# First feed-forward tile prepared inside the last mixing batch, and the last Fourier parts dealt one tile later

## The chip, the cores and the metric

The kernel runs on one core of one Trainium2 chip. The metric is device time in microseconds of one launch, as the median of three runs. A profile of one execution gives the busy time of each engine: TensorE (PE, with its weight loads as PEld), VectorE (DVE), ScalarE (ACT), GpSimd (POOL), and the DMA queues that SyncE (SP), ACT and POOL issue to.

## The reference, cut to what matters

```python
# q, k, v: (8, 12, 448, 64) float32; w_pre, w_post: (12, 12)
scores = q @ k^T / 8
scores = einsum('bhij,hg->bgij', scores, w_pre)      # mix heads
attn   = softmax(scores, axis=-1)
attn   = einsum('bhij,hg->bgij', attn, w_post)       # mix heads again
x      = (attn @ v) as (8, 448, 768)
u      = x + real(fft(fft(x, axis=1), axis=2))
un     = (u - mean(u)) / sqrt(var(u) + 1e-6)         # per row of 768
out    = u + relu(un @ w_ch1) @ w_ch2                # 768 -> 3072 -> 768
```

The feed-forward weights arrive as 64-bit floats and are turned to 32-bit ones in the kernel. The 8 x 448 = 3584 rows of `u` are 7 feed-forward tiles of 512 rows.

## The kernel before, in words

**Mixing.** `mix_phase` runs over 8 batches of 23 steps, 184 in all. A step takes rows of scores (`Kr`, gathered from `Sb` by SP, L496), mixes heads on PE (premix, L507, into `mx`), takes the maximum (DVE, L514), the exponential (ACT, L521), scales (POOL, L531, two steps ahead of its use), mixes heads again on PE (postmix, L541, into `po`) and transposes on DVE (L554). Products QK (L479) and AV (L571) are interleaved. The attention output of a batch is transposed to rows `X` (L615, PE), folded on POOL (`fold`, L636 to L657: sums and differences of `X` into `xf`), transformed in two products (`emit_z`, L680; `emit_s2`, L696), added to `X` on DVE (L707, L709) and stored as `u` in two scratch tensors, `u_scr` in order and `u_rev` reversed (SP L728, POOL L719, L725). A tile's rows thus come from up to four stretches of a batch.

**What orders the mixing.** `due(kind, step, fn)` puts a piece of work on one of four lists; the main loop takes from them at fixed places of each step (`ORDERS`). Kind "none" is taken at the head of a step, "full" late in it. PE, DVE, ACT and POOL keep this order (`manual_schedule`). A function of kind "none" that returns a true value, as the loads of q and k do, lowers the number of folds in that step from two to one. The last batch begins at step `f = 161`. The loop ends at step 190, and eight Fourier pieces of the last batch (four `z`, four `s2`) with a last flush are left over: they are handed to the next phase as nine `parts`. Raw q and k lie in the pool `praw` (4 buffers), their transposes in `pqt` (4 of `qT`, 4 of `kT`), and PSUM tiles `ms` come from four banks.

**Feed-forward.** `ffn_phase` runs over six chunks `c` of the hidden width and over the seven tiles `t` in each (n = 7c + t); a chunk is computed by a seven-product scheme. `first(n)` has seven steps of 12 products (L1062) into `psP`, `psQ`, `psR`; `second(n)` has seven of 8 products (L1135) for the first two chunks. A tile is loaded (`load_u`, L946), its statistics are taken on DVE (`stats`, L971), the power -0.5 on POOL (`power`, L976 to L979), it is normalised on ACT (`norm`, L987), turned by 24 PE transposes (`turn`, L996, evacuated in L1003) into four half tiles `ub`, and three more `ub` are differences of those (`total`, L1008). Seven `ub` of each tile are stored for later chunks (L1012). For tile 0 all of this stands ahead of `first(0)`; for tile t + 1 it is spread over `first(t)` and `second(t)`. Between tile 0's power and its `norm`, `fold_rest` issues on POOL what folding the last batch has left. `next_part` runs one of the nine parts: before, after five of the seven steps of `first(0)` and after steps of `second(0)`.

**Weights.** `_Weights` converts pieces of the weights: a raw load on POOL (L225), seven DVE operations (L247 to L273), stores (L233). Loads run `ahead` pieces ahead: 4 in the feed-forward phase, with 5 buffers.

**Memory.** Pools of the mixing end with it, and those of the feed-forward phase lie over them: `pub` (11 buffers for `ub`), `pw1`, `pw2`, `ph`, the weight pools, `pun`, and `pu` (3 buffers of 512 rows). PSUM: two banks each for Q, P and R, and two for the leftover parts (`ppx`), which become a third pair (`ppy`) when the parts are done.

Of the kernel before, what the change touches and what calls it, by code (L numbers as in the profile page):

```python
# [16 lines left out]
P = 128  # L17
# [47 lines left out]
C7 = 7  # L65
# [234 lines left out]


@with_exitstack
def mix_phase(ctx, tc, rest, ident, q, k, v, w_pre, w_post, u_scr, u_rev, wts):

# [7 lines left out]
    def pool(name, bufs=1, **kw):  # L312
        return ctx.enter_context(tc.tile_pool(name=name, bufs=bufs, **kw))
# [3 lines left out]

    praw = pool("praw", 4)
    pqt = pool("pqt", 4)
    psb = pool("psb", 2)  # L320
# [415 lines left out]
    def due(kind, at, fn):  # L736
        fill[kind].append((at, len(fill[kind]), fn))
# [4 lines left out]
    for b in range(B):  # L742
# [38 lines left out]
        for pair in range(2):  # L781
            for par in range(2):
                due("full", f + AT_S[pair][par],
                    lambda b=b, pair=pair, par=par: emit_s2(b, pair, par))
    due("none", 0, lambda: wts.deal(0))
    due("none", -39, emit_load_mix)
# [87 lines left out]
OPENS = (0, 1, 4)  # L874
ORDER2 = (0, 3, 5, 6, 4, 1, 2)
DEEP = 2
DEALS = ((0, 2, 2, 2, 2, 0, 0), (2, 3, 3, 3, 3, 0, 0))
# [5 lines left out]
def ffn_phase(ctx, tc, rest, ident, u_scr, u_rev, wts, ub_scr, out, fold_rest,  # L883
              parts):

# [7 lines left out]

    pub = pool("pub", 11)
    pw1 = pool("pw1", 7)
    pw2 = pool("pw2")
    ph = pool("ph")
    wts.open(ctx, tc, 4)
    once = ExitStack()
# [5 lines left out]
    pun = early("pun", 2)  # L905
    pu = early("pu", 3)
    pps = [pool("pps" + k, space=bass.MemoryType.PSUM) for k in "QPR"]
# [16 lines left out]
    def next_part():  # L924
        if parts:
# [6 lines left out]
           for t in range(NTB) for r in range(2) for d in range(2)}  # L932
    mhalf = pst.tile([P, NT2], F32, name="mhalf", bufs=1)
    nc.gpsimd.memset(mhalf[:, :], -0.5)

    def load_u(t):
        us[t] = pu.tile([P, NT2, DM], F32, name="u", tag="u")
        for x in range(NT2):
            p = 0
            while p < P:  # L940
                b, r = divmod(t * TB + x * P + p, S)
                k = sum(r >= e for e in ENDS)
                n = min(P - p, ENDS[k] - r)
                src = (u_rev if k % 2 else u_scr)[b]
                for p0, m in _split(p, n):
                    nc.sync.dma_start(out=us[t][p0:p0 + m, x, :],  # L946
                                      in_=src[r + p0 - p:r + p0 - p + m, :])
                p += n

# [8 lines left out]
    def new_ub(n, i):  # L958
        ubs[n, i] = pub.tile([P, NK, HT], F32, name="ub", tag="ub")


    UB = {(0, 0): 0, (0, 1): 6, (1, 0): 1, (1, 1): 2}

    mvs, uns = {}, {}

    def stats(t, x):
        if x == 0:
            mvs[t] = pst.tile([P, NT2, 3], F32, name="mv", tag="mv", bufs=2)
        st = pst.tile([P, 2, 6], F32, name="st", tag="st")
        for y in range(2):  # L970
            nc.vector.bn_stats(st[:, y, :], us[t][:, x, y * DH:(y + 1) * DH])  # L971
        nc.vector.bn_aggr(mvs[t][:, x, 0:2], st[:, :, :])

    def power(t):
        var = mvs[t][:, :, 1]
        nc.gpsimd.tensor_scalar(var, var, 1e-6, None, op0=ALU.add)  # L976
        nc.gpsimd.tensor_tensor(var, var, mhalf[:, :], op=ALU.pow)
        nc.gpsimd.tensor_tensor(mvs[t][:, :, 2], mvs[t][:, :, 0], var, op=ALU.mult)
        nc.gpsimd.tensor_scalar(mvs[t][:, :, 2], mvs[t][:, :, 2], -1.0, None,  # L979
                                op0=ALU.mult)  # L980

    def norm(t, x):
        if x == 0:
            for i in (0, 6, 1, 2, 4, 5, 3):
                new_ub(t, i)
        uns[x] = pun.tile([P, DM], F32, name="un", tag="un")
        nc.scalar.activation(uns[x][:, :], us[t][:, x, :], ACTF.Identity,  # L987
                             bias=mvs[t][:, x, 2:3], scale=mvs[t][:, x, 1:2])

    def turn(t, x):  # L990
        un = uns.pop(x)
        for y in range(2):
            ps = ps_tile("Q")
            for c in range(NK):
                cc = NK * y + c
                tr = nc.tensor.transpose(ps[:, c * P:(c + 1) * P],  # L996
                                         un[:, cc * P:(cc + 1) * P], ident[:, :])
                if t == x == y == c == 0:

                    tc.keep_in_program_order(tr)  # L1000

            copy = nc.vector.tensor_copy if t == 0 and y else nc.scalar.copy
            copy(out=ubs[t, UB[y, x // 2]][:, :, (x % 2) * P:(x % 2 + 1) * P],  # L1003
                 in_=ps[:, :NK * P].rearrange("p (c n) -> p c n", n=P))

    def total(t, n):
        o, a, b = ((4, 6, 0), (5, 2, 4), (6, 2, 6), (3, 1, 5))[n]
        nc.vector.tensor_tensor(ubs[t, o][:, :, :], ubs[t, a][:, :, :],  # L1008
                                ubs[t, b][:, :, :], op=ALU.subtract)
        if n == 3:  # L1010
            for i in ORDER:
                nc.sync.dma_start(out=ub_scr[t][i], in_=ubs[t, i][:, :, :])  # L1012

# [23 lines left out]
    def first(n, st, beside):  # L1037
# [12 lines left out]
        for k, i in enumerate(ORDER):  # L1050
# [6 lines left out]
            for m in range(FM):  # L1057
                for kc in range(NK):
                    for fn in beside.pop(done, ()):
                        fn()  # L1060
                    done += 1
                    nc.tensor.matmul(p[:, m, :], w1[i][:, kc, m * P:(m + 1) * P],  # L1062
                                     ub[:, kc, :],
                                     start=i in (0, 4, 1)[:3 - seed] and m == kc == 0,
                                     stop=kc == NK - 1, skip_group_check=True)
            if i == 0 and seed:
# [21 lines left out]
            else:  # L1088
                nc.scalar.activation(h12, p, ACTF.Relu)
            if norms and k < NT2:  # L1090
                stats(t + 1, k)
                if k == NT2 - 1:
                    power(t + 1)
            if n == 0 and k not in (1, 2):
                next_part()
# [23 lines left out]
    def second(n, st):  # L1119
# [9 lines left out]
        for k, i in enumerate(ORDER):  # L1129
            for x in range(NT2 // 2):  # L1130
# [9 lines left out]
                if c == 0:  # L1140
                    us_ = u[:, 2 * r + x, d * DH:(d + 1) * DH]
                    nc.vector.tensor_tensor(us_, us_, p, op=ALU.add)
                    if last:
                        nc.sync.dma_start(out=acc[t, r, d][:, x, :], in_=us_)
                    continue
# [17 lines left out]
            if norms and k >= NT2 - 1:  # L1163
                total(t + 1, k - NT2 + 1)
            if n == 0:
                next_part()
# [109 lines left out]

    for t in range(2):
        load_u(t)
    for i in ORDER:
        load_w1(0, i)  # L1280
    ET = mybir.EngineType
    with tc.manual_schedule(engines={ET.PE, ET.DVE, ET.Pool}):
        for x in range(NT2):
            stats(0, x)
        power(0)
        fold_rest()
    with tc.manual_schedule(engines={ET.PE, ET.DVE}):
        for x in range(NT2):
            norm(0, x)
            turn(0, x)  # L1290
        for i in ORDER:
            load_w2(0, i)
        for n in range(4):
            total(0, n)
        parts_ = [(c, k) for c in range(1, NC) for k in range(NK + FM)]
        for n in range(DEEP * NTB):
            c, t = divmod(n, NTB)
            if c == 0 and 0 < t < NK + FM + 1:
                wts.add(*parts_.pop(0))
            while c and sum(o[1] for o in wts.ops) < 52:  # L1300
                wts.add(*parts_.pop(0))
            wts.deal(0)
            if n + 2 < NTB:
                load_u(n + 2)
            st = {}
            first(n, st, {})
            second(n, st)
            if c == 0:
                wts.deal(1000)
            if n == 0:  # L1310
                assert not parts
                rest.close()
                beside.close()
                pps.append(pool("ppy", space=bass.MemoryType.PSUM))
            if n == NTB - 1:
                once.close()
                for name, bufs in (("wt", 1), ("hq", 1), ("od", 9)):
                    right[name] = pool("p" + name, bufs, side="right")
# [29 lines left out]
def kernel(  # L1348
# [19 lines left out]
    ub_scr = [scr.tile([7, P, NK, TB // 2], F32, name=f"ub_{t}") for t in range(NTB)]  # L1368
    wts = _Weights(nc, moe_w_ch1, moe_w_ch2, scr)
    rest = ExitStack()  # L1370
    fold_rest, parts = mix_phase(tc, rest, ident, q, k, v, w_pre, w_post, u_scr, u_rev,
                                 wts)
    ffn_phase(tc, rest, ident, u_scr, u_rev, wts, ub_scr,
              out.rearrange("b s d -> (b s) d"), fold_rest, parts)

# [30 lines left out]
```

## Time and profile before

| what | us |
|---|---|
| median of 3 runs (lowest to highest) | 2374.74 (2374.28 to 2377.43) |
| the profiled execution, whole | 2376.62 |
| its span, first to last instruction | 2374.9 |
| mixing: last matmul ends | 820.7 |
| first product of the feed-forward phase (L1062) starts | 845.6 |
| `second(0)` starts (L1135 in the chain) | 883.4 |
| `first(1)` starts | 908.6 |
| `second(1)` starts | 926.7 |

How to read it: the page gives busy time by engine over the span and in 40 slices of 59.4 us. The first feed-forward tile falls into slices 14 to 16. A group's row gives a line, its engine, what it writes and reads, and the mean time of one instruction; a wait is put down to what came last before the waiting instruction.

### The profile page before, as it was taken

The numbers are of one execution on the slowest core, as the hardware profiler recorded it, in microseconds if no ns is written. First come the engines' busy times: TensorE is split into PE (matmuls) and PEld (weight loads), VectorE is DVE, ScalarE is ACT, GpSimd is POOL, SyncE is SP. The second block draws the span as 40 slices with busy tenths as digits, with TensorE's granted clock in tenths as the row PEclk, the third lists the DMA queues.
The fourth block names the chain that finished last, engine by engine and source line by source line (L and its number), as shares of the span: only waits on it lengthen the run. The fifth ranks groups of instructions, "written<-read, shape, count | busy, mean of one in ns | idle before, by whom it ended". The sixth has DMA issues, their size and how long they took to land.

```text
span 2374.9 us, 59455 instructions
## 1 busy us (share of the span) xinstructions
PE 2282.5 (96%) x22600; PEld 1716.0 (72%) x22600; DVE 1677.3 (71%) x3596; ACT 1102.4 (46%) x3085; POOL 1130.8 (48%) x1680
## 2 busy tenths in 40 slices
PE   6999999999999769999999999999999999999998
PEld 2455555555555457767777779999899999999997
DVE  3768877787877547786676766778767777776556
ACT  4766766666676422222122224443444444344444
POOL 3587867878777341121234443335333433443333
PEclk9999999999999979999999999999999999999999
DMA  7565555656645636666888895569456846674553
GB/s 160 156 181 175 174 178 154 202 160 181 189 148 171 216 106 205 193 217 239 229 238 231 206 299 140 147 168 272 128 140 180 238 129 178 167 221 113 147 128 66
DMA packets 213625, 425.60 MB, mean 179 GB/s; under 512 B 39014, under 2 KB 135678, under 8 KB 213342
## 3 DMA queue, kind: packets, MB, share of 16 engines
q1 hardware_dynamic: 142430, 280.35, 34.4%
q0 software_dynamic: 64912, 139.48, 27.0%
q8 instruction: 181, 2.97, 0.5%
q10 hardware_dynamic: 6000, 1.97, 0.5%
q14 instruction: 102, 0.84, 0.1%
HBM read 213.16 MB, written 129.39 MB: 144 GB/s over the span
## 4 chain that ended last, share of the span: by engine, by line
PE 76%; issue 7%; DMA 5%; POOL 4%; DVE 4%; ACT 3%; SPq 1%; ACTq 0%; POOLq 0%; DVEq 0%
PE psP L1062 15%; PE psP L1192 10%; PE psR L1062 8%; PE mx L507 6%; PE psR L1192 5%; PE ms L571 5%; PE ms L479 5%; PE psQ L1062 4%; PE po L541 4%; PE psP L1135 4%; DMA Kr<-Sb 3%; PE psQ L1192 2%; PE psR L1135 2%; PE ms L696 2%; ACT PP L521 1%
## 5 line engine op out<-in xcount | busy, mean ns | idle before, releaser
L1062 PE MATMUL psP<-ub,w1t 128*128 128x256 f32 x2016 | 480.5, 379 | 1.3 <-DVE h L1081 1.3
L1062 PEld LDWEIGHTS psP<-ub,w1t 128*128 128x128 f32 x2016 | 379.0, 190 | 49.5 <-DVE h L1081 1.7
L531 POOL TENSOR_SCALAR PP<-PP,rcp 128x448 f32<-128x448 f32 x368 | 234.5, 647 | 214.7 <-DVE rcp L529 172.7
L521 ACT ACTIVATE PP<-mx,nmx 128x448 f32<-128x448 f32 x368 | 230.3, 631 | 189.6 <-DVE nmx L514 177.4
L514 DVE TENSOR_REDUCE nmx<-mx 128x1 f32<-128x448 f32 x368 | 214.1, 619 | 134.8 <-PE mx L507 132.1
L1226 POOL DMA_DIRECT2D out_dram<-od x109 | 133.1, 1427 | 281.9 <-DVE od L1223 159.5
L1026 POOL TENSOR_TENSOR hq<-h 128x256 f32<-128x256 f32 (+1 forms) x168 | 104.6, 622 | 291.0 <-ACT h L1082 171.6
L1062 PE MATMUL psR<-ub,w1t 128*128 128x256 f32 x1008 | 232.9, 381 | 0.0
L507 PE MATMUL mx<-Kr,kw 60*32 60x448 f32 x2944 | 213.4, 550 | 14.1 <-DMA Kr<-Sb 12.3
L1223 DVE TENSOR_TENSOR od<-od 128x768 f32<-128x768 f32 x196 | 188.9, 975 | 52.5 <-ACT od L1220 50.7
L1062 PEld LDWEIGHTS psR<-ub,w1t 128*128 128x128 f32 x1008 | 192.6, 191 | 26.4
L479 PE MATMUL ms<-kT,qT 64*32 64x448 f32 (+1 forms) x3072 | 202.4, 547 | 9.3 <-ACT qT L342 6.6
L554 DVE STREAM_TRANSPOSE Pv<-po 128x896 f32<-128x896 f32 x184 | 203.7, 1107 | 7.5 <-PE po L541 3.7
L342 ACT COPY Sb<-ms 124x448 f32<-124x448 f32 (+1 forms) x384 | 184.4, 540 | 39.5 <-PE ms L479 24.5
L541 PE MATMUL po<-PP,kw 60*32 60x448 f32 x2944 | 197.1, 541 | 0.3 <-DVE rcp L528 0.2
L1220 ACT COPY od<-psP 128x192 f32<-128x192 f32 x390 | 124.7, 320 | 145.5 <-PE psP L1192 141.1
L571 PEld LDWEIGHTS ms<-Pv,vv 64*64 64x64 f32 x5376 | 137.4, 132 | 69.0 <-issue 48.9
L225 POOL DMA_DIRECT2D raw<-in_moe_w_ch_dram x88 | 53.2, 605 | 262.9 <-DVE tmp L269 256.8
L571 PE MATMUL ms<-Pv,vv 64*64 64x120 f32 (+1 forms) x5376 | 159.2, 263 | 0.4 <-ACT PP L521 0.4
L1135 PE MATMUL psP<-w2t,h 128*128 128x384 f32 x448 | 153.7, 486 | 0.0
L1081 DVE TENSOR_TENSOR h<-h,psP 128x512 f32<-128x512 f32 x42 | 28.8, 687 | 141.5 <-PE psP L1062 141.2
L1135 PEld LDWEIGHTS psP<-w2t,h 128*128 128x128 f32 x448 | 84.1, 190 | 53.1
(144 smaller groups left out, 4506.8 us busy)
## 6 DMA issues: line engine op xcount, KB each, us to landing
ub<-ub SPq DMA_DIRECT2D x294, 384.0 KB
Kr<-Sb SPq DMA_DIRECT2D x736, 105.0 KB
out_dram<-od POOLq DMA_DIRECT2D x137, 384.0 KB, 7.0
w1t<-w SPq DMA_DIRECT2D x42, 384.0 KB
w2t<-w SPq DMA_DIRECT2D x42, 384.0 KB
raw<-in_moe_w_ch_dram POOLq DMA_DIRECT2D x56, 256.0 KB, 4.1
raw<-in_moe_w_ch_dram POOLq DMA_DIRECT2D x32, 384.0 KB, 4.4
w<-wst POOLq DMA_DIRECT2D x92, 128.0 KB, 3.5
```

Of the source, the lines that this page charges most:

```text
L479: nc.tensor.matmul(pss[x][o:o + hi - lo, :S], st["qT", xx][64 * x:64 * x + 64, y, lo:hi], st["kT", xx][64 * x:64 * x + 64, y, :], start=Tr ...
L507: nc.tensor.matmul(mx[x][64 * z + o:64 * z + o + 32, :S], kw1[64 * x:64 * x + KR, o:o + 32], Kr[64 * x:64 * x + KR, z, :], start=True, sto ...
L514: nc.vector.tensor_reduce(nmx[:, :], steps[T]["mx"][x][:, :S], axis=AX.X, op=ALU.max, negate=True)
L521: nc.scalar.activation(steps[T]["PP"][:, x, :], steps[T]["mx"][x][:, :S], ACTF.Exp, bias=steps[T]["nmx", x][:, :], accum_out=steps[T]["den ...
L531: nc.gpsimd.tensor_scalar(PP[:, x, :], PP[:, x, :], rcp[:, x:x + 1], 1.0, op0=ALU.mult, op1=ALU.mult)
L541: nc.tensor.matmul(po[o:o + 32, z, :S], kw2[64 * z:64 * z + KR, y, :], PP[64 * z:64 * z + KR, :, c * HS:(c + 1) * HS], start=True, stop=True)
L554: nc.vector.transpose(turned[a]["Pv"][:, j, :].rearrange("p (z s) -> p z s", z=2), steps[T]["po"][:, :, :S])
L571: nc.tensor.matmul(pss[y][64 * x:64 * x + 64, :nu * R], st["v", pr][64 * y:64 * y + 64, x, jb * D:(jb + 1) * D], _ap(Pv, 64 * y * rp + 32 ...
L1062: nc.tensor.matmul(p[:, m, :], w1[i][:, kc, m * P:(m + 1) * P], ub[:, kc, :], start=i in (0, 4, 1)[:3 - seed] and m == kc == 0, stop=kc == ...
L1135: nc.tensor.matmul(p, h[:, LHS[i], kf, x * P:(x + 1) * P], w2[i][:, kf, :], start=i in (0, 4, 1)[:3 - (c > 0)] and kf == 0, stop=kf == FM ...
L1192: nc.tensor.matmul(ps[j, key][:, :DQ], a, b, start=m in (0, 4), stop=True, skip_group_check=True)
L1223: eng.tensor_tensor(D[j][:, :, :], D[j][:, :, :], D[k][:, :, :], op=ALU.add)
```

## The change

A new class `_Lead` owns the pools `praw` and `pqt` (now opened for the whole kernel and used by the mixing as before) and does for tile 0 what `load_u`, `stats`, `power`, `norm`, `turn` and `total` did: within the last mixing batch, put on the lists by `due`.

- Loads of tile 0: from POOL instead of SP, 12 DMAs, at the head of steps 162 to 169, into `praw` buffers.
- Statistics at steps 169 to 172, power at 173, `norm` at 175, 176, 180, 181, `turn` at 179, 181, 183, 185 (through the mixing's `ms` tiles), three of the four differences at 187 to 189. Normalised rows and six `ub` lie in `pqt`, the seventh in `pub`.
- Ahead of `first(0)` remain the last difference and `fold_rest`. Loads of tile 1 are issued after those of the first weights `w1`; stores of tile 0's `ub` come after the loads of `w2`.
- `pub` has 3 buffers, and later `ub` rotate over 4 + 4 of `pqt` and these 3. `pu` has 2 buffers, and every third tile's rows lie in `praw`. Weight loads run 3 pieces ahead, in 4 buffers.
- Parts: none in `first(0)`; four after steps 3 to 6 of `second(0)`, five in `first(1)`. The extra PSUM pair and the mixing's right-hand pools change hands after tile 1 instead of tile 0. In `first(0)` statistics of tile 1 come three steps later.

The diff, cut to its core:

```diff
+class _Lead:
...
+    def ub_tile(self, pub):
+        kind = "qkqkqkqkxxx"[self.at % 11]
+        self.at += 1
+        if kind == "x":
+            return pub.tile([P, NK, TB // 2], F32, name="ub", tag="ub")
+        return self.as_ub(kind)
...
+    def load(self, x, half):
+        if half == 0:
+            self.u.append(self.rows())
+        ps = list(_u_pieces(0, x, *self.scr))
+        n = (len(ps) + 1) // 2
+        for p0, m, src in ps[half * n:half * n + n]:
+            self.nc.gpsimd.dma_start(out=self.u[x][p0:p0 + m, :], in_=src)
+
+    def stats(self, x):
+        st = self.st[x % 2]
+        for y in range(2):
+            self.nc.vector.bn_stats(st[:, y, :], self.u[x][:, y * DH:(y + 1) * DH])
+        self.nc.vector.bn_aggr(self.mv[:, x, 0:2], st[:, :, :])
...
+    def norm(self, x):
+        self.un[x] = _flat(self.slot("qk"[x % 2]), DM)
+        self.nc.scalar.activation(self.un[x], self.u[x], ACTF.Identity,
+                                  bias=self.mv[:, x, 2:3], scale=self.mv[:, x, 1:2])
+
+    def turn(self, x, tile_fn):
...
+        for y in range(2):
+            ps = tile_fn()
+            for c in range(NK):
+                cc = NK * y + c
+                self.nc.tensor.transpose(ps[:, c * P:(c + 1) * P],
+                                         un[:, cc * P:(cc + 1) * P], self.ident[:, :])
+            copy = self.nc.vector.tensor_copy if y else self.nc.scalar.copy
...
@@ mix_phase
-    praw = pool("praw", 4)
-    pqt = pool("pqt", 4)
+    praw, pqt = lead.praw, lead.pqt
...
+    f = (B - 1) * GS
+    due("none", f, lambda: nc.gpsimd.memset(lead.mhalf[:, :], -0.5))
+    for x in range(TB // P):
+        for y in range(2):
+            due("none", f + 1 + 2 * x + y, lambda x=x, y=y: lead.load(x, y))
+        due("none", f + 8 + x, lambda x=x: lead.stats(x))
+        due("none", f + (14, 15, 19, 20)[x], lambda x=x: lead.norm(x))
+        due("full", f + 18 + 2 * x, lambda x=x: lead.turn(x, ms_tile))
+    due("none", f + 12, lambda: lead.power(lead.mv))
+    for n in range(3):
+        due("none", f + 26 + n, lambda n=n: lead.total(n))
@@ ffn_phase
-    pub = pool("pub", 11)
+    pub = pool("pub", 3)
-    wts.open(ctx, tc, 4)
+    wts.open(ctx, tc, 3)
-    pu = early("pu", 3)
+    pu = early("pu", 2)
@@ first
-            if norms and k < NT2:
-                stats(t + 1, k)
-                if k == NT2 - 1:
+            x = k - 3 * (n == 0)
+            if norms and 0 <= x < NT2:
+                stats(t + 1, x)
+                if x == NT2 - 1:
                     power(t + 1)
-            if n == 0 and k not in (1, 2):
+            if n == 1 and k not in (1, 2):
                 next_part()
@@ second
-            if n == 0:
+            if n == 0 and k > 2:
                 next_part()
@@ the loop over tiles
-    for t in range(2):
-        load_u(t)
     for i in ORDER:
         load_w1(0, i)
+    load_u(1)
+    us[0] = lead.u
     with tc.manual_schedule(engines={ET.PE, ET.DVE, ET.Pool}):
-        for x in range(NT2):
-            stats(0, x)
-        power(0)
+        lead.total(3, pub)
         fold_rest()
+    for i in ORDER:
+        ubs[0, i] = lead.ub[i]
     with tc.manual_schedule(engines={ET.PE, ET.DVE}):
-        for x in range(NT2):
-            norm(0, x)
-            turn(0, x)
         for i in ORDER:
             load_w2(0, i)
-        for n in range(4):
-            total(0, n)
+        store_ub(0)
...
-            if n == 0:
+            if n == 1:
                 assert not parts
                 rest.close()
                 beside.close()
```

## The prediction

> **What bounds the kernel now.** I read the page first, for the engine that carries the span and for slices in which it doesn't.
>
> ```profile
> PE 2282.5 (96%) x22600; PEld 1716.0 (72%) x22600; DVE 1677.3 (71%) x3596; ACT 1102.4 (46%) x3085; POOL 1130.8 (48%) x1680
> ...
> PE   6999999999999769999999999999999999999998
> ...
> PEclk9999999999999979999999999999999999999999
> ```
>
> TensorE is busy in every slice but two, the 14th and 15th of 59.4 us each: the seam between the last mixing batch and the first feed-forward tile. A table of stretches (length, then busy us of PE, PEld, DVE, ACT, POOL, then granted clock, DMA share, GB/s) cuts it up.
>
> ```profile
> 802.00:817.00 15.00, 14.69 (x324) 11.68 (x318) 8.54 (x18) 4.05 (x23) 2.30 (x3) 1.00 0.87 306
> 817.00:820.80 3.80, 1.98 (x28) 1.54 (x20) 0.75 (x3) 1.55 (x7) 2.22 (x4) 1.00 0.81 255
> 820.80:839.90 19.10, 0.02 (x1) 0.02 (x1) 4.91 (x12) 1.96 (x4) 5.03 (x10) 0.60 0.91 236
> 839.90:848.40 8.50, 8.42 (x36) 6.11 (x36) 4.27 (x7) 4.63 (x8) 8.11 (x10) 0.69 0.17 67
> 848.40:860.20 11.80, 0.00 (x0) 0.00 (x0) 5.71 (x12) 0.54 (x1) 11.33 (x16) 0.65 0.89 303
> 860.20:883.40 23.20, 22.89 (x113) 20.19 (x114) 7.22 (x14) 6.87 (x11) 4.58 (x7) 0.88 0.03 10
> ```
>
> PE stands still twice, 19.1 and 11.8 us, and works in between and afterwards at a granted clock of 0.69 and 0.88. The chain of waits (start, us, what) says on what:
>
> ```profile
> 818.81 1.46 SPq L946
> 820.33 8.07 DMA u<-v
> ...
> 838.51 0.26 POOL mv L979
> 838.77 1.92 POOL xs L636 x2
> ...
> 859.25 1.91 POOL xf L657 x2
> 861.20 1.44 PE ms L680 x6
> 862.64 4.15 PE psR L1062 x12
> ```
>
> First hole: the rows of tile 0 load only from 818.4 (their memory is the mixing's, free after the last AV), then statistics, the power on POOL, normalising, turning. Second hole: POOL is in order, so the last batch's folds start behind that power, at 838.7, and run to 863; the first Fourier part (L680), dealt after the first step of `first(0)`, waits for them and holds every product behind it.
>
> **The change, part by part.** I sum one stretch: from the last mixing matmul (820.7) to the end of `first(1)`, where `second(1)` starts in the chain (926.7): 106.0 us before. The same parts lie within it afterwards, so their move from tile 0 to tile 1 cancels, but for holes.
>
> Its work at full clock, from later rows of the chain: `first`, 7 steps of 12 products at 2.59 = 18.13 each, twice 36.26; `second(0)`, 7 steps of 8 at 2.58 = 18.06; turning of tile 1, 4 x 0.655 (6 transposes) = 2.62; Fourier, 4 x 0.78 (L680) + 4 x 1.31 (L696) = 8.36. Sum 65.3. So holes, slow clock and the turning of tile 0 are worth 106.0 - 65.3 = 40.7 us. This uses measured full-clock durations, so the clock's loss is in it once.
>
> *Turning in the batch.* 24 transposes return in the mixing at 2.62 us. PE is 14.68 to 15.00 of every 15 us busy there, so I count all of it, though a drain hole (1.8 of the 3.8 us at 817) might take some: 38.1 left.
>
> *12 tile loads on POOL, moved off SP.* From 727 to 756 (steps 162 to 169) 1, 1, 2, 2, 2, 2, 1, 1 are issued, ahead of the scaling (L531) of the step two later, which releases postmix (L541). No row shows them on POOL. Near ones: whole-row weight loads (L225) 0.56 us median, V loads (L434) 0.63; I take 0.6. POOL has one gap of 2.91 us before 730.7 and then next to none till 744.5, since the folds of batch 6 run there, two a step: loads of `_Lead` return nothing and don't halve them as q and k loads did. Walking the queue: scaling 168, done 749.93, is wanted by postmix at 751.30 (slack 1.4). By then 7 loads lie in front that no earlier gap takes: 7 x 0.6 - 0.57 (gap at 744.5) - 1.4 = 2.2 us late; for step 170 the slack is 5.6 and POOL has caught up. PE then waits for a gather of rows (Kr, 0.9 us) anyhow, so I take 1.3. Low end 0 (later waits absorb it). [...] But the row decides: 42 V loads from POOL land 4.0 to 5.4 us after issue with VectorE 6 to 8 tenths busy, and hold POOL 0.66 at most. I take 0.6 and keep 5.0 as high end.
>
> *Their 1.57 MB beside the gathers.* DMA share is 0.53 at 727 to 742 and 0.79 at 742 to 757 (170, 222 GB/s). 1.57 MB in 29 us adds 54 GB/s, towards the 300 seen at the seam. Kr gathers are on the chain there (7.42 us). Batch 6, with q and k loads beside it, is nearest: PE waited 1.1 us once for Kr at 643, batch 5 1.7. I take 1.0, bounds 0 and 3. V loads are queued behind the tile loads on POOL: wanted from 765, so covered.
>
> *Statistics, normalising, evacuation.* DVE: 4 x 1.23 + 4 x 0.56 + 3 x 0.96 = 10 us over steps 169 to 189, where it is busy 6 to 8 tenths; ACT 4 x 1.03 + 4 x 0.48 = 6 us at 5 to 8 tenths; POOL's power 1.8 us at 772, where gaps of 0.6 to 2.6 follow. All lie beside PE, but DVE and ACT are in order and reductions or exponentials queue behind them for a microsecond. Taken 0.7; bounds 0 and 3.
>
> *The seam.* `first(0)` needs the tile (the last sum but one lies before the end of mixing), w1 (issued 796.4; now over memory of gathers, last read 801, so landed some 10 us early) and PSUM (psR two steps after the last evacuation). Folds: last X copied at 823.2, shifted by about 5; 24.3 us of folding as seen (838.7 to 863.0) ends near 853; the first Fourier part now comes after four steps of `second(0)`, at 826.3 (820.7 + 2.6 + 3.0 of the three costs above) + 18.1 + 4 x 2.58 + 2.6 = 857. Hidden, by 4 us only; what folding lacks beyond that is paid in full. w2 went out at 807 and is wanted at 844. The loads of tile 1 now head the queue once the last AV lets their memory go (818 to 823); its statistics, put three steps later, come near 834. Then `store_ub(0)`, 7 issues in 8.84 us: tile 1's turned tiles take tile 0's buffers in the q and k pools (the rotation meets them after 7, where before four fresh ones were left), so the first evacuation, near 847, waits for stores that should end near 838. Taken 1.0 in all; bounds 0 and 10.
>
> *`first(1)` and the rest.* Five parts there add 5.7 us of VectorE work (3 x 4 x 0.47) to 11.1 of 18.1; the spare PSUM pair comes one tile later. 1.0; bounds 0 and 3. One weight load less in flight: a piece is 7 VectorE operations dealt 2 to 4 a step, so three pieces are 21 / 4 x 2.59 = 13.6 us or more ahead, and loads land in 4.4 us (10.8 at most): 0. Third rows buffer now in the raw pool, reuse distance unchanged: 0.
>
> Sum: 38.1 - 1.3 - 1.0 - 0.7 - 1.0 - 1.0 = 33.1. The profiled execution took 2376.62 (span 2374.9, 1.7 around it), 1.9 above the median of 2374.74; the saving carried over to the median gives 2341.6. All low ends: 2336.6; a drain hole filled too: 2334.
>
> **The rivals.**
> *One wait takes another's place* (stores of tile 0's turned tiles, or w2, late behind the tile-1 loads): the DMA engines stood at 0.81 to 0.91 while PE stood still. Stores one transfer train (8.84) late would give about 2350. Against: from 820.8 to 926.7 they moved 16.6 MB (rates times lengths of the stretches); 15 MB without tile 0, in 71 us, is 211 GB/s, under the 303 seen.
> *POOL becomes the bound in the batch*: at 1.43 us a load, as accumulating stores (L1226) cost, lateness is 7 x 1.43 - 2.0 = 8 us, and folds slip past 857: about 2350.
> *It doesn't do what it says*: if folds or a mistimed w1 still hold PE, the second hole (11.8) stays: 2353.
> *Slower*: the shallower weight look-ahead, over all 100 pieces of the later chunks. From the point where a load takes longer than three pieces of dealing (13.6 us), every piece stalls VectorE and PE behind it; 0.38 us each loses 38 us, and the time is 2380. Nothing shown lands past 10.8.
>
> **How the numbers follow.** Main case 0.66 (own range 2335 to 2347); new wait 0.14; POOL 0.09; hole stays 0.06; slower 0.03; no difference 0.02, from combinations. Two in ten are left out at 2334 to 2352. A measurement tells about 0.2% (4.7 us) from no change: faster 0.95, same 0.02, slower 0.03.
>
> **What would show it.** PE row without the 7 and 6, PEclk 9 throughout; no loads of tile 0 from SP at 818; transposes within steps 179 to 185; L680 in `second(0)` after xf with no wait. Wrong if PE waits for L531 or Kr at 745 to 760 for over 4 us, if evacuations of tile 1 wait for DMA of ub, or if VectorE waits for raw.

## The result, and the profile after

The changed kernel takes 2359.0 us (median of 10 runs, 2352.3 to 2370.9) where the kernel before took 2375.2 on the same chip (10 runs, 2370.4 to 2382.9): a ratio of 0.9933 [0.9914, 0.9952], 16.2 us or 0.67% less. The forecast was 33.1 us less. The direction is right, half of the gain is missing, and the time lies outside the range. The profiled execution took 2356.8 us, its span is 2355.1.

The page's busy times and its rows of slices for TensorE and its clock, after:

```profile
PE 2286.6 (97%) x22600; PEld 1717.5 (73%) x22600; DVE 1673.8 (71%) x3596; ACT 1103.0 (47%) x3085; POOL 1138.8 (48%) x1692
...
PE   6999999999999989999999999999999999999998
...
PEclk9999999999999999999999999999999999999999
```

The 7 and 6 are gone; an 8 stays in the 15th slice. PE is busy 4.1 us longer for the same 22600 matmuls. The same table of stretches as before, of after: the last batch from postmix (L650 now) of step 161 to that of step 183, the drain to the first product, `first(0)`, `second(0)`, `first(1)`:

```profile
718.22:810.64 92.42, 86.71 (x1669) 47.77 (x1653) 66.26 (x140) 59.25 (x183) 65.48 (x103) 0.98 0.56 168
810.64:830.72 20.08, 16.17 (x287) 13.66 (x287) 12.83 (x22) 5.49 (x25) 13.64 (x15) 0.93 0.94 354
830.72:849.05 18.33, 18.33 (x85) 16.11 (x85) 6.00 (x13) 4.20 (x8) 13.84 (x21) 0.99 0.97 257
849.05:881.81 32.76, 27.88 (x114) 18.25 (x112) 16.14 (x29) 9.09 (x15) 3.29 (x5) 0.90 0.30 112
881.81:904.68 22.87, 22.87 (x118) 20.63 (x117) 16.25 (x39) 6.55 (x10) 5.53 (x8) 1.00 0.47 147
```

And the kernel before, cut at the same places (the batch, and the drain up to its last matmul):

```profile
722.89:805.49 82.60, 81.84 (x1657) 44.90 (x1641) 60.67 (x126) 55.12 (x177) 57.48 (x86) 1.00 0.54 174
805.49:820.73 15.24, 13.18 (x275) 10.88 (x274) 6.93 (x16) 4.24 (x22) 3.27 (x5) 1.00 0.84 285
```

`first(0)` starts 20.1 us behind the last postmix, where it started 40.1 behind, and takes 18.3 where it took 37.7: both holes of the kernel before are closed. Against that stand 9.8 us more in the batch (PE is busy 4.9 longer there, of which 1.6 are transposes of tile 0), 4.8 more in the drain, and a `second(0)` of 32.8 us with 4.9 in which PE does nothing, at a clock of 0.90. Aligned at step 161, the way to the first product of `first(2)` is 208.4 us against 225.4: 17.0 saved, which agrees with the medians. The profiled spans differ by 19.8, but that execution was 4.7 us ahead before the last batch began, and lost 1.8 at a later boundary of chunks. `second(1)` and the stages behind it are as before (21.98 us against 21.74).

The waits of PE in that stretch, by its line and what came last (us in total, times, longest):

```profile
PE psQ L1105 <- ACT un L1096: 4.3, 1, 4.3
PE ms L724 <- DVE XT L713: 3.2, 1, 3.2
PE mx L616 <- DMA Kr<-Sb: 3.1, 1, 3.1
PE po L650 <- issue: 1.8, 1, 1.8
```

Four places, one in `second(0)` (turning tile 1), one in the drain, two in the batch. None is one of the evacuations, stores or late weights that the forecast named.

### The profile page after: what moved, and what is told of

Its sections match the earlier page's. It is cut to its first block, busy times and chain, and to the rows that moved or that the text cites. A ratio compares the mean times of both kernels' runs of the same rounds, so it can differ in the third digit from the quotient of the medians.

```text
span 2355.1 us, 59472 instructions
## 1 busy us (share of the span) xinstructions
PE 2286.6 (97%) x22600; PEld 1717.5 (73%) x22600; DVE 1673.8 (71%) x3596; ACT 1103.0 (47%) x3085; POOL 1138.8 (48%) x1692
## 3 DMA queue, kind: packets, MB, share of 16 engines
q0 software_dynamic: 65440, 141.05, 27.4%
## 4 chain that ended last, share of the span: by engine, by line
PE 57%; DVE 3%; issue 2%; DMA 1%; POOL 1%; ACT 0%; SPq 0%; POOLq 0%; DVEq 0%
PE psP L1169 17%; PE psP L1302 10%; PE psR L1169 9%; PE psR L1302 5%; PE psP L1245 5%; PE psQ L1169 4%; PE psR L1245 3%; PE psQ L1302 3%; PE psQ L1245 1%; PE psQ L1105 1%; DVE hq L1133 1%; DMA w<-wst 0%; DMA u<-u 0%; DMA w2t<-w 0%; POOL w L233 0%
## 5 line engine op out<-in xcount | busy, mean ns | idle before, releaser
L640 POOL TENSOR_SCALAR PP<-PP,rcp 128x448 f32<-128x448 f32 x368 | 234.8, 647 | 207.0 <-DVE rcp L638 165.0
L650 PE MATMUL po<-PP,kw 60*32 60x448 f32 x2944 | 196.1, 543 | 2.0 <-issue 1.8
L680 PEld LDWEIGHTS ms<-Pv,vv 64*64 64x64 f32 x5376 | 137.7, 132 | 70.6 <-issue 50.1
L1169 PE MATMUL psP<-qs,w1t 128*128 128x256 f32 x744 | 177.4, 379 | 0.0
L1169 PE MATMUL psP<-ks,w1t 128*128 128x256 f32 x744 | 176.9, 379 | 0.3 <-DVE h L1190 0.2
L680 PE MATMUL ms<-Pv,vv 64*64 64x120 f32 (+1 forms) x5376 | 160.2, 263 | 0.6 <-ACT X L451 0.3
L1169 PEld LDWEIGHTS psP<-ks,w1t 128*128 128x128 f32 x744 | 139.9, 190 | 19.0 <-DVE u L1252 0.7
L1169 PEld LDWEIGHTS psP<-qs,w1t 128*128 128x128 f32 x744 | 140.0, 190 | 17.4
L1169 PE MATMUL psP<-ub,w1t 128*128 128x256 f32 x528 | 126.4, 379 | 0.0
```

The costliest lines, as they stand in the source:

```text
L640: nc.gpsimd.tensor_scalar(PP[:, x, :], PP[:, x, :], rcp[:, x:x + 1], 1.0, op0=ALU.mult, op1=ALU.mult)
L650: nc.tensor.matmul(po[o:o + 32, z, :S], kw2[64 * z:64 * z + KR, y, :], PP[64 * z:64 * z + KR, :, c * HS:(c + 1) * HS], start=True, stop=True)
L680: nc.tensor.matmul(pss[y][64 * x:64 * x + 64, :nu * R], st["v", pr][64 * y:64 * y + 64, x, jb * D:(jb + 1) * D], _ap(Pv, 64 * y * rp + 32 ...
L1169: mm = nc.tensor.matmul(p[:, m, :], w1[i][:, kc, m * P:(m + 1) * P], ub[:, kc, :], start=i in (0, 4, 1)[:3 - seed] and m == kc == 0, stop= ...
```

## The experiments

All times of stretches are aligned as above; "to `first(2)`" runs from postmix of step 161 to the first product of `first(2)`. One correction holds for the texts on record below: they take 87.9 us for the batch and 203.9 to `first(2)` in the changed kernel. There a postmix that PE interrupts (753.74 and 756.46, with a wait between) had been counted as two steps. Counted once they are 92.4 and 208.4, and the spread of 85.7 to 90.8 quoted in one text is 90.2 to 92.4.

| kernel | batch | drain | `first(0)` | `second(0)` | `first(1)` | to `first(2)` |
|---|---|---|---|---|---|---|
| before | 82.6 | 40.1 with the first hole | 37.7 with the second, and parts | 25.2 | 18.1 | 225.4 |
| changed | 92.4 | 20.1 | 18.3 | 32.8 | 22.9 | 208.4 |
| changed, once more (e11) | 91.8 | 19.8 | 18.1 | 33.6 | 22.9 | 208.2 |
| statistics earlier (e1) | 90.2 | 20.0 | 19.8 | 30.0 | 22.9 | 204.8 |
| tile loads earlier (e2) | 84.0 | 20.4 | 19.8 | 28.9 | 22.9 | 197.9 |
| tile loads from SP, and earlier (e3) | 83.5 | 20.2 | 19.0 | 33.2 | 22.9 | 200.7 |
| differences later (e4) | 90.6 | 17.0 | 18.1 | 34.2 | 22.9 | 204.8 |
| folds off POOL (e10) | 90.4 | 21.0 | 18.4 | 30.6 | 22.9 | 205.2 |
| e1 and folds off POOL (e8) | 90.8 | 19.5 | 19.7 | 25.4 | 22.9 | 200.3 |
| e1, e2, e4, e8 (e9) | 84.2 | 16.7 | 18.1 | 25.4 | 22.9 | 189.3 |

My theory after the result: POOL's order delays the batch, the differences delay the drain, and late statistics delay `second(0)`. The rivals: the tile's bytes compete with the gathers, and a saturated DMA (share 0.94 to 0.97 at the seam) brings the rows of tile 1 too late whatever the order.

**The hole in `second(0)`: e1, e10, e8.** In the changed kernel it reads so (start, us, engine, line; in brackets the idle time before and what ended it):

```profile
851.35 1.00 DVE L1085 BATCH_NORM_STATS2 st<-u 128x6 f32<-128x384 f32 x2
852.39 0.21 DVE L1086 BATCH_NORM_AGGREGATE mv<-st 128x2 f32<-128x12 f32 x1
852.70 0.56 POOL L375 TENSOR_SCALAR mv<-mv 128x4 f32<-128x4 f32 x1 [2.42 <-DVE mv L1086]
853.34 1.05 POOL L376 TENSOR_TENSOR mv<-mv,mhalf 128x4 f32<-128x4 f32 x1
855.04 1.94 ACT L1096 ACTIVATE un<-u,mv 128x768 f32<-128x768 f32 x2 [5.19 <-POOL mv L378]
856.12 1.11 PE L1105 MATMUL psQ<-ident,un 128*128 128x128 f32 x4 [4.32 <-ACT un L1096]
```

The fourth statistic comes after the last step of `first(0)`; power, normalising and turning follow it one behind the other, and the turn is ahead of products on PE. e1 takes the statistics two steps earlier:

```diff
-            x = k - 3 * (n == 0)
+            x = k - 1 * (n == 0)
```

> Statistics of tile 1 begin one step into first(0) instead of three, so the last of the four comes at its fifth step instead of its seventh. Theory A (the new wait in second(0) is the chain last statistics, power, normalise, turn, which the change puts two to three steps later; the rows have long landed): first(0) stays at 18.3 us, second(0) shrinks from 32.8 to about 25 us, the time falls by 7 to 8.5 us against the changed kernel. Theory B (tile 1's rows land late because the DMA engines stand at 0.9 to 1.0 from 810 to 850 us): VectorE then waits for the rows ahead of its additions, first(0) grows by what second(0) loses, and the time falls by less than 3 us.

Measured: `second(0)` 30.0, 204.8 to `first(2)`; 2359.9 us, ratio 0.9909 [0.9886, 0.9932] to the kernel before on its chip. Neither theory held as written. The wait moved instead of going away (e1, timeline):

```profile
850.99 3.88 POOL L766 TENSOR_TENSOR xf<-xq 113x385 f32<-113x385 f32 x4
851.73 0.21 DVE L1086 BATCH_NORM_AGGREGATE mv<-st 128x2 f32<-128x12 f32 x1
854.96 0.25 POOL L375 TENSOR_SCALAR mv<-mv 128x4 f32<-128x4 f32 x1
857.00 1.03 ACT L1096 ACTIVATE un<-u,mv 128x768 f32<-128x768 f32 x1 [5.58 <-POOL mv L378]
858.46 0.57 ACT L1198 ACTIVATE h<-psP 128x512 f32<-128x512 f32 x1
859.08 2.93 PE L1245 MATMUL psP<-w2t,h 128*128 128x384 f32 x4 [2.65 <-ACT h L1198]
```

The statistics are done at 851.9, but the power is in POOL's queue behind the last folds and starts at 854.96. ACT, in order too, holds `norm` ahead of the activations of `h` (L1196, L1198), for which the next products wait 2.65 us: what L1196 reads is done at 853.3 (L1195), and it starts behind `norm`, at 857.94. So there is a second cover: POOL's folds. e10 puts the folds of the last batch's second pair of groups on VectorE and leaves the statistics where the change put them; e8 does both:

```diff
-        pl = nc.gpsimd
+        pl = nc.vector if pair and g["b"] == B - 1 else nc.gpsimd
```

> The changed kernel with the folds of the last half batch on VectorE, statistics of tile 1 left where the change puts them. If statistics and folds are two covers one behind the other, each enough to hold the power: taking the folds off POOL alone gains nothing there, second(0) stays at 31 to 33.5 us and PE waits about 4 us for tile 1's normalised rows. If the folds alone hold the power: second(0) falls to 26 us or less.

> As the run with statistics from the first step on, and in addition the folds of the last half batch (12 pieces, 14 us on POOL) run on VectorE, which stands idle for 12 us there. Theory C (what holds tile 1's normalising is its power, queued on POOL behind the folds): the power follows the last statistics within 3 us, normalising starts some 3 us earlier than there, second(0) shrinks from 30.0 to 25 to 26.5 us, and first(0) stays under 20. Theory B (rows of tile 1 land late): second(0) stays above 28 us, or first(0) grows over 21.

Measured: e10 30.6 with a wait of 3.3 us before the turn (2359.6 us, 0.9921 [0.9901, 0.9942]); e8 25.4 with none over 0.3 (2354.9 us, 0.9894 [0.9866, 0.9921]). Either edit alone takes 2.2 to 2.8 us, both take 7.3 (two traces of the changed kernel differ by 0.8): two covers one behind the other, each enough to hold PE. This is against the rival of saturated DMA: in e8 the DMA share is 0.91 in the drain and 0.96 in `first(0)`, and PE has its 25.4 all the same. VectorE did wait in e1 for rows of tile 1, 3.2 and 3.0 us, but nothing of PE hung on that.

**The batch: e2, e3.** POOL in the changed kernel, 745 to 753:

```profile
745.17 0.71 POOL L543 DMA_DIRECT2D vv<-in_v_dram  x1
745.88 1.07 POOL L365 DMA_DIRECT2D ur<-u  x2
746.98 1.26 POOL L640 TENSOR_SCALAR PP<-PP,rcp 128x448 f32<-128x448 f32 x2
748.43 1.04 POOL L828 DMA_INDIRECT v<-X,rows  x1 [0.19 <-issue]
749.47 0.69 POOL L543 DMA_DIRECT2D vv<-in_v_dram  x1
750.16 1.03 POOL L365 DMA_DIRECT2D ur<-v  x2
751.22 1.27 POOL L640 TENSOR_SCALAR PP<-PP,rcp 128x448 f32<-128x448 f32 x2
752.42 1.29 POOL L543 DMA_DIRECT2D vv<-in_v_dram  x2
```

Two tile loads (L365) and a V load (L543) lie ahead of each scaling (L640), back to back. e2 issues the loads from step 156 to 161, where POOL still has gaps; e3 leaves their steps in the program and issues them from SP:

```diff
-            due("none", f + 1 + 2 * x + y, lambda x=x, y=y: lead.load(x, y))
+            due("none", f - 5 + 3 * (2 * x + y) // 4, lambda x=x, y=y: lead.load(x, y))
```

```diff
-            self.nc.gpsimd.dma_start(out=self.u[x][p0:p0 + m, :], in_=src)
+            self.nc.sync.dma_start(out=self.u[x][p0:p0 + m, :], in_=src)
```

> The 12 loads of tile 0 go out at steps 156 to 161 instead of 162 to 169, where POOL has gaps of 2.6 to 3.4 us a step and the DMA share is 0.29 to 0.43. Theory A (the last batch is stretched by the loads, on POOL and beside the gathers): from the postmix of step 161 to that of 183 it takes about 84 us instead of 87.9 (82.6 before the change), the wait for Kr near 766 (3.1 us) and the late scaling near 754 go, and the time falls by about 4 us. Theory B (statistics and normalising, which sit ahead of the reductions and exponentials in their queues, stretch it): it stays within 1 us of 87.9, and the time doesn't move.

> The 12 loads go out at the same steps from SP instead of POOL: POOL is relieved of 6.4 us, the bytes stay. If POOL's queue is the cost: postmix of step 168 is on time (now 2.4 us late), the wait for Kr near 766 is under 1.5 us too, and steps 161 to 183 take about 84.5 us. If the bytes beside the gathers are the cost: postmix 168 is on time, but PE still waits about 3 us for Kr, and steps 161 to 183 take 86.5 us or more.

Measured: the batch takes 84.0 and 83.5 us (e2, with columns as in the stretches above):

```profile
727.59:811.55 83.96, 83.26 (x1669) 46.89 (x1653) 66.06 (x140) 58.94 (x183) 59.77 (x92) 1.00 0.54 173
```

e2 timed 2357.5 us, 0.9893 [0.9872, 0.9914]; e3 was timed once, 2364.2, so only its stretches are read. e2 shows that the place of the loads costs 8.5 us (6.2 to 8.5 over the seven traces with late loads, whose batches took 90.2 to 92.4). e3 was meant to part POOL's queue from the bytes, and does not: SP is not among the engines that keep the order of the steps, and its loads went out 37 to 16 us ahead of postmix of step 161 (733.81), where those of the changed kernel go out 5 to 42 us behind it (718.22). Half of the loads, `ur<-u`, by line (durations in ns as lowest, median, highest, then first and last start), e3 and changed:

```profile
L365 SPq DMA_DIRECT2D ur<-u x6: 273/412/1538, 697.0 to 717.8; - x6
L365 POOL DMA_DIRECT2D ur<-u x6: 503/535/568, 723.1 to 760.2; - x6
```

So e3 is a second test of an earlier place, with a cost ahead of the stretch: between postmix of steps 158 and 160 it lost 2.4 us on the kernel before, with a wait of 1.4 for `Kr`, which the table leaves out. e2 lost nothing there.

Two things can be seen at work, POOL's queue and slower transfers; their shares are not separated. How lateness grows shows in the starts of postmix against those of before, from step 161 on: 168 is 2.4 us late (the forecast said 2.2), 169 2.8, 170 4.7, 171 7.5, 172 8.6, 183 9.8. In e3 step 168 is on time (28.42 us after step 161 against 28.41). The lateness isn't absorbed: PE waits for scaling, then for V or for gathered rows. The exact place changes from run to run. In the changed kernel it is a postmix (L650; the trace names no cause) and Kr; in e11, the same program, it is also AV (L680), in front of which nothing was to stand:

```profile
753.36 0.99 PE L650 MATMUL po<-PP,kw 60*32 60x448 f32 x16 [0.57 <-POOL PP L640]
761.29 1.70 PE L680 MATMUL ms<-Pv,vv 64*64 64x120 f32 x54 [1.60 <-DMA vv<-in_v_dram]
769.81 1.85 PE L616 MATMUL mx<-Kr,kw 60*32 60x448 f32 x16 [4.41 <-issue]
```

Six of the seven traces with late loads on POOL show that wait for V, of 0.8 to 2.8 us (e1, e4, e6, e8, e10, e11; not that of the changed kernel). In the kernel before the V load in question goes out 28.3 us behind postmix of step 161 and lands after 5.4 us, 1.3 ahead of the AV that reads it (757.86). In the six it goes out at 31.2 or 31.3, since more stands ahead of it on POOL, and lands after 6.6 to 9.4 us; the wait ends within 0.2 us of that. The chain in e4 (start, us, what):

```profile
748.59 0.71 POOL vv L543
749.30 1.07 POOL ur L365 x2
...
751.85 1.04 POOL v L828
752.89 8.80 DMA vv<-in_v_dram
```

Landing after 5.4 us it would have been there at 36.7, and AV started between 36.0 and 39.0: by this estimate the slower landing makes most of that wait. The DMA share from 30 to 46 us behind step 161 is 0.82 in the changed kernel, 0.56 before and 0.53 in e2. Whether the bytes slow it, or the DMA queue of POOL, which the tile loads share with V (q0 on the page, 141.05 MB against 139.48 before), no run shows.

**The drain: e4.** VectorE takes the three differences before the small memset of `XT`, and the last transposes of `X` need that. The first (820.60) fills a gap; the next two stand directly ahead of the memset. The fourth (827.82), left ahead of `first(0)`, starts beside it (changed kernel, VectorE, then PE):

```profile
820.60 0.95 DVE L408 TENSOR_TENSOR qs<-ks,qs 128x768 f32<-128x768 f32 x1
...
825.12 1.50 DVE L408 TENSOR_TENSOR ks<-ks,qs 128x768 f32<-128x768 f32 x1
826.54 1.34 DVE L408 TENSOR_TENSOR ks<-ks 128x768 f32<-128x768 f32 x1
827.82 1.33 DVE L408 TENSOR_TENSOR ub<-qs,ks 128x768 f32<-128x768 f32 x1
827.84 0.06 DVE L713 MEMSET XT<- 128x6 f32 x1
```

```profile
828.05 2.87 PE L724 MATMUL ms<-ident,XT 128*113 128x128 f32 x12 [3.17 <-DVE XT L713]
```

e4 puts all three on step 190, behind the memset:

```diff
-        due("none", f + 26 + n, lambda n=n: lead.total(n))
+        due("none", f + 29, lambda n=n: lead.total(n))
```

> The three differences on VectorE (1.3 to 1.5 us each there) are issued at step 190 instead of 187 to 189, behind the small memset that the last transposes of X wait for. Theory A (the differences ahead of that memset hold PE in the drain): PE's wait before the last transposes falls from 3.2 us to under 1, the stretch from the last postmix to the first product of first(0) shrinks by 2 to 3 us, and so does the time. Theory B (the additions into X and the copy of XT set the memset's time): it doesn't move by more than 0.7 us.

Measured: the drain takes 17.0 us, 3.1 less, and the wait is 0.8. But `second(0)` grows from 32.8 to 34.2, with a wait of 6.3 us before the turn. Here the other cover ended last: the statistics were done at 850.2, and the power started behind the folds at 853.3. 2359.0 us, 0.9907 [0.9882, 0.9932].

**One half alone: e5, e6.** e5 is the kernel before with only the parts moved (`n == 1` for those of `first`, `k > 2` for those of `second(0)`); e6 is the changed kernel with the parts put back:

```diff
-            if n == 1 and k not in (1, 2):
+            if n == 0 and k not in (1, 2):
...
-            if n == 0 and k > 2:
+            if n == 0:
```

> The kernel before with the second half of the change alone: no Fourier parts in first(0), four from the fourth step of second(0), five in first(1); tile 0 is still prepared after the mixing. From the postmix of step 161 to the first product of first(2) the kernel before takes 225.4 us, the changed one 203.9. Theory: the second standstill (11.8 us, with some 2 us of slow clock) goes, and about 1 us of it comes back as a wait of tile 1's power behind the folds on POOL: 212 to 214 us. Rival (folds merely hold the part at its new place, in second(0)): 219 us or more.

> The changed kernel with the first half alone: tile 0 prepared in the last batch, but the Fourier parts at their old places in first(0). Theory: the first part waits after one step of first(0), near 834 us, for the folds that end near 850, some 15 us; this covers the wait for tile 1's power, which ends at the same folds, so second(0) has no hole: the stretch from postmix 161 to first(2) is 211 to 215 us instead of 203.9. Rival (folds start at once and are done in time): 206 us or less.

Measured to `first(2)`: 217.5 for e5 and 216.3 for e6, savings of 7.9 and 9.1, which add up to the 17.0 of both. Timed, 2372.2 us, 0.9974 [0.9959, 0.9990], and 2370.1, 0.9966 [0.9949, 0.9983]. e5 saves less than its text expected (212 to 214); e6 is 7.9 us above the changed kernel, within the 7 to 11 of its text. e5 kept the first hole, and got a `second(0)` of 32.1 in which the power again waits behind the folds; e6 waits 13.7 us in `first(0)` for `xf`, which is the second hole of the kernel before come back.

**All four removed: e9, e12.** e9 joins the edits of e1, e2, e4 and the folds line of e8; e12 is e9 and e11 the changed kernel, once more and on one chip.

> All four together: loads of tile 0 at steps 156 to 161, differences behind the memset, statistics of tile 1 from the second step on, folds of the last half batch on VectorE. If the four costs are separate: steps 161 to 183 84 us, drain 17, first(0) 18.2 to 19, second(0) 25 to 26, so 190 us from postmix 161 to first(2) instead of 203.9, and a time 12 to 14 us below the changed kernel (about 0.6% more). If they hide one another (a seam that comes earlier meets the same landing of tile 1's rows): 195 us or more.

> The changed kernel itself, unaltered, for a comparison on one chip with the version of all four edits, and for a second trace of its last batch: with the loads in the batch on POOL, steps 161 to 183 have taken 85.7 to 90.8 us in five traces, so a value between these, first(0) 18 to 20, second(0) 32 to 34 us.

> The version of all four edits again, beside the changed kernel: 0.5 to 0.7% below it (traces: 189.3 against 203.9 us from postmix 161 to first(2)). If its gain came from the chip or the day, not from the edits: within 0.2% of it.

The stretches of e9 up to the end of `second(0)` (columns and cuts as above):

```profile
723.84:807.99 84.15, 82.36 (x1669) 46.19 (x1653) 66.16 (x140) 58.83 (x183) 59.82 (x92) 1.00 0.53 171
807.99:824.72 16.73, 14.56 (x287) 12.33 (x287) 9.88 (x20) 4.92 (x24) 10.18 (x12) 1.00 0.89 341
824.72:842.86 18.14, 18.14 (x87) 15.97 (x86) 15.28 (x34) 4.87 (x9) 7.67 (x12) 1.00 0.95 294
842.86:868.27 25.41, 24.85 (x114) 16.62 (x112) 14.66 (x26) 8.49 (x16) 0.00 (x0) 1.00 0.51 176
```

189.3 us to `first(2)` (e12: 189.5), a clock of 1.00 throughout, and 0.6 us in which PE stands still in `second(0)`. e9 timed 2349.0, 0.9881 [0.9856, 0.9907]; e12 2345.5, 0.9869 [0.9851, 0.9886]; e11 2361.7, 0.9940 [0.9925, 0.9955]. On that one chip the version without the four costs is 30.1 us below the kernel before and 16.2 below the changed kernel. The stretch itself saves 36 in the profiled executions, which were the fastest of their kernel's runs (2341.3 of e9, 2340.4 of e12, medians 2349.0 and 2345.5); why the other runs are slower stays open.

## Why the prediction was wrong

The base was right: the two holes and the slow clock behind them were worth what the sum said (40.7 us less the 3.2 of turning is 37.5, and e9, without the costs that follow, saves 36.1), and `first(0)` ran without a wait right behind the drain. What was mis-sized, term by term, over the batch, the drain, and the way to the end of `first(1)`:

| term | forecast | measured | from |
|---|---|---|---|
| turning tile 0 in mixing | 2.62 | 3.2 | 24 transposes, 4 x 0.80 from start to next start |
| tile loads on POOL | 1.3 | 8.5 with the next | 92.4 - 84.0 (e2) |
| their bytes beside the gathers | 1.0 | in the 8.5 | not separated |
| statistics, normalising, evacuation | 0.7 | about 0 (-0.2) in the batch | 84.0 - 82.6 - 1.6 |
| differences ahead of the memset | in the 0.7 | 3.2 | 20.1 - 15.2 - 1.6; e4 takes 3.1 of it |
| seam, in `second(0)` | 1.0 | 8.4 | 32.8 - 24.3 of its work (18.06 + 2.62 + 3 x 0.78 + 1.31) |
| `first(0)` | 0 | 0.2 | 18.3 - 18.1 |
| `first(1)`, parts on VectorE | 1.0 | 0 | 22.9 - 22.8 |

The sum of the differences is 15.7 us; 33.1 less 17.0 is 16.1.

- *The price of a load on POOL was right, its place was not.* Loads held POOL 0.49 to 0.57 us (0.6 taken), and step 168 was late by about what the walk of the queue gave: 2.4 us here, 1.7 in the six other traces, which is the walk's sum at 0.53 a load (7 x 0.53 - 2.0). The walk stopped there. The step that failed is "for step 170 the slack is 5.6 and POOL has caught up", with "V loads are queued behind the tile loads on POOL: wanted from 765, so covered": postmix 170 was 4.7 us late and 171 7.5. And V was misread: the AV that needs it starts at 757.9 in the kernel before, 1.3 us after V has landed, and not at 765. That V loads land 4.0 to 5.4 us after issue held for the six of 42 whose landing the trace has, without tile loads beside them; with these, the V load in question took 6.6 to 9.4. No run shows a price of a load that gives the 5.0 us of the high end: no load held POOL for over 0.57 us, and the loss (8.5 us in the batch) was in the followers. The sign that the forecast set itself, over 4 us of waits for L531 or Kr at 745 to 760, showed in kind: 1.8 in a postmix, for which the trace names no cause, and 3.1 for Kr at 763.
- *"All lie beside PE" failed for the differences.* They are in the forecast's sum for VectorE (the 3 x 0.96), at steps where VectorE had room. Room was not the question: the memset behind them releases PE, and two of them took 1.50 and 1.34 us ahead of it.
- *"Its statistics, put three steps later, come near 834"* costed the first of four. The last is at 852.4 and two engines follow it. That the power sits on POOL behind the folds was not seen either: the folds were held against the Fourier parts alone. The first part did come after the folds without a wait, as said.
- *Weights.* No wait of VectorE for raw weights showed, so the shallower look-ahead costs nothing here, as taken. The evacuations of tile 1 never waited for stores.
- *The rivals.* "One wait takes another's place" happened in kind, in `second(0)`, but with another cause: statistics and power, not stores. "POOL becomes the bound in the batch" came true in size (8.5 us against 8) at little over a third of the price that it named (0.53 us a load against 1.43), so not by its mechanism. "It doesn't do what it says" and "slower" fell.

The range was too narrow because each unknown cost had a high end of its own, and the main case took all of them near their low ends, where POOL's order tied them together: it holds the tile loads, the V loads and the power.

## What to carry to other kernels

When work is put on an in-order queue that feeds a bound engine, walk every follower on that queue to its consumer, and don't stop at the first slack: 12 loads of 0.53 us, with their bytes, cost 8.5 us in one place, and next to nothing some six steps earlier (e2: a batch of 84.0 us against 82.6, with 1.6 of transposes in it). When an edit leaves the order to an engine that is not held to it, read in the trace when it acted. Of a chain that is moved, time its last element (last statistic, power, normalise, turn), and list all that stands behind it on each engine, a small memset included. When removing one cover changes little, look for a second one behind it, and test the two together.

## What the runs showed of the hardware

- *Some waits were followed by a slower clock, others of the same length were not.* After 3.17 us without work the last 12 transposes of `X` took 2.87 us in the changed kernel, at a granted clock of 0.50, against 1.56 in e9 after a wait of 0.81. The loss varies with the same wait: in e1, after 3.14, the clock was 0.50 over the next 4.5 us, and `first(0)` took 19.8 us, 1.7 longer than in e9; in e11, after 3.16, the transposes took 1.54 and the steps of `first(0)` 2.75 each, as in e9, and nothing was lost:

```profile
833.53 1.54 PE L724 MATMUL ms<-ident,XT 128*113 128x128 f32 x12 [3.16 <-DVE XT L713]
```

In `second(0)` of the changed kernel 4.3 us of waiting were followed by a clock of 0.78 over 857 to 868: PE was busy 27.9 us in `second(0)`, 3.0 longer than in e9. A shorter wait had a loss behind it too: in e1, after 2.65 us (859.08), four products took 2.93 us where the four ahead of the wait took 1.45, and the six transposes behind them 1.13 where later ones took 0.82. What decides whether a wait is followed by a loss, no run shows.

- *Differences on VectorE and folds on POOL took longer beside each other.* In the changed kernel a difference of 128x768 took 1.33 to 1.50 us on VectorE beside POOL's folds (from 825.12), and 0.95 or 0.96 later, with POOL at rest (L1112); a pair of POOL's quarters took 2.45 beside them (825.88) and 1.15 with VectorE at rest (840.29). It did not go both ways each time: the difference at 820.60 took 0.95 beside a pair of quarters that took 1.79. The cause, no run shows.
- *The folds ran twice as fast on VectorE*: a pair of the first additions took 1.01 us (L745, e9) against 1.96 on POOL (changed kernel), and `first(0)` was no longer for the move (18.4 us in e10, 18.3 in the changed kernel).
